# Moving the low parts of the first layer's inner values, group 0, from GpSimd to VectorE

## The chip, the cores and the metric

The kernel runs on one core of a Trainium2 chip. A core has five engines that work side by side, each through its own queue in order: TensorE (PE in the profile, with its weight loads as PEld), VectorE (DVE), ScalarE (ACT), GpSimd (POOL) and SyncE (SP), which here issues nearly all transfers. The metric is the device time of one execution in microseconds (us). Before the change it is 747.45 us, the median of three runs (747.26 to 748.68).

## The reference

Three stages follow each other on 1152 tokens of width 512:

```python
# attention: 2 batches, 8 heads, 576 positions, head width 64
scores = scale * q @ k.T
scores = where(scores >= max(scores) - tau, scores, -1e9)
x = softmax(scores) @ v                                   # laid out as 1152 x 512
# first layer: inner width 768
h = maximum(maximum(x @ w1, x @ w2), x @ w3)
x = h @ w_out
# experts: 4 of them, inner width 1024, weighted by normalised domain_probs
out = sum(p[:, e] * (maximum(x @ w1[e], 0) @ w2[e]) for e in range(4))
```

The change lies in the first layer: `h` is the "inner value" of its title.

## The kernel before

Every product is made from split operands. A 32-bit value `v` is cut into a high part `hi` (a copy in the type fp32r) and a low part `lo = v - hi`, and a product is the sum of three matrix products, `hi*lo`, `lo*hi` and `hi*hi` (`split_term`). So each weight block and each activation tile needs a copy (the high part, on ScalarE) and a subtraction (the low part).

The tokens are cut into two groups. Group 0 holds 512 tokens of batch 0, group 1 the other 640, worked in two halves of 320. The program runs attention on batch 0, then the layers of group 0 as one long stream of products (`Stream`), into which attention on batch 1 is woven towards the end of the first layer, then the layers of group 1.

In the first layer of group 0 the outer loop runs over six blocks `f` of 128 inner columns, and for each over the three weight matrices `i = 0, 1, 2`. One block of weights is 128x512 (four slices of 128x128) and takes 12 matrix products of 512 columns on TensorE; the first `f` is worked in two halves of 256 tokens. Then the output matrix follows, four output blocks `d` with two weight blocks of 128x384 each.

The weights come as 64-bit floats, and each block is turned into 32-bit by integer work in the same stretch (`block`): L648 loads the words; ScalarE scales the upper word (L656); GpSimd clamps it (L666, tile `b`); VectorE takes three bits of the lower word (L663), merges them with the clamped word (L669) and sets the sign (L674, tile `raw`). After that ScalarE copies the high part (L633, tile `a`), GpSimd makes the low part (L637, tile `a`), and SyncE keeps the 32-bit block in device memory for group 1 (L680). Four word tiles are in flight.

After each block of products, `after_max` takes the running maximum: for `i = 0` ScalarE copies the sums (L718), for `i = 1` and `2` VectorE takes the maximum of the new sums in PSUM and the old maximum in SBUF (L720, tile `hmax`). After `i = 2` two more steps follow: ScalarE copies the high part (L725, tile `hh`) and the low part is made from `hmax` and `hh` (L728, tile `hl`). Both `hmax` and `hh` lie in SBUF. The products with the output matrix read `hh` and `hl`.

What sets the order: weights' steps are planned at a lag, in columns of products, ahead of their use (`LAGS64`, `LAGS_FIRST`), and the steps after a block are put 1000 columns apart behind it (`AFTER`). In this stretch the engines' orders are those in which the stream calls the steps (`ordered`). When the last words have been used, their memory is given to attention on batch 1, whose first loads (`load_job`, L129 and L130) stand on SP's queue behind the last L680.

Of the kernel before, what the change touches and what calls it, by code (L numbers as in the profile page):

```python
# [14 lines left out]
ALU = mybir.AluOpType  # L15
# [6 lines left out]
def fused_kernel(ctx: ExitStack, tc: tile.TileContext, q, k, v, tau, w1, w2, w3, w_out, probs, m_w1, m_w2, out):  # L22
    nc = tc.nc
# [47 lines left out]
    def f32(ap):  # L71
        return ap.bitcast(F32)
# [365 lines left out]
    class Queue:  # L438
# [3 lines left out]
        def add(self, gen):  # L442
            self.q.append(gen)
# [164 lines left out]
    def htile(g, nm):  # L608
        return mo["h"].tile([P, GROUPS[g]["n"]], F32R, tag="h", name=nm, bufs=HB[g])

    def wtile(shape, dt, tag, bufs):
        return wp.tile(shape, dt, tag=tag, name=tag, bufs=bufs)
# [74 lines left out]
    def block64(w, cols):  # L687
        return w.bitcast(U32).rearrange("(k p) (f two) -> p k f two", p=P, two=2)[:, :, cols, :]

    def weights64(g, name, use, src, shape):  # L690
        kept["planned"] = kept.get("planned", 0) + 1
        return block(use, shape, "a", NA, None, (LAGS_FIRST if kept["planned"] <= EARLY else LAGS64, LAGS_KEPT)[g], name, g, src if g == 0 else None)
# [13 lines left out]
    def layer_max(g):  # L706

        G = GROUPS[g]
        hs = [None] * NF
        acc = {}  # L710

        def after_max(f, i, si, a, z):
            def first(ps):
                if hs[f] is None:
                    hs[f] = (htile(g, "hh"), htile(g, "hl"))
                new = wtile([P, z - a], F32, "hmax", 3)
                if i == 0:
                    nc.scalar.activation(out=new, in_=ps, func=AF.Copy)  # L718
                else:
                    nc.vector.tensor_tensor(out=new, in0=ps, in1=acc[si], op=ALU.max)  # L720
                acc[si] = new

            def hi(ps):
                acc["done", f, si] = acc[si]
                nc.scalar.activation(out=hs[f][0][:, a:z], in_=acc[si], func=AF.Copy)  # L725

            def lo(ps):
                nc.gpsimd.tensor_tensor(out=hs[f][1][:, a:z], in0=acc["done", f, si], in1=f32(hs[f][0][:, a:z]), op=ALU.subtract)  # L728

            return [first, hi, lo] if i == 2 else [first]  # L730

        for f in range(NF):

            halves = [(0, MAIN // 2), (MAIN // 2, MAIN)] if g == 0 and f == 0 else []
            bs = {}
            for i, (si, (a, z)) in [(i, s) for s in enumerate(halves) for i in range(3)] or [(i, s) for i in range(3) for s in enumerate(G["subs"])]:
                if i not in bs:
                    bs[i] = weights64(g, f"w{i}_{f}", plan.cols, block64((w1, w2, w3)[i], slice(f * P, (f + 1) * P)), [P, KC, P])
                add(z - a, KC, lambda j, b=bs[i], a=a, z=z: (
                    b["hi"][:, j, :], b["lo"][:, j, :], X[g][j][0][:, a:z], X[g][j][1][:, a:z]), after_max(f, i, si, a, z))  # L740
        K2 = NF // 2
        for d in range(KC):
            bs = []
            for i in range(2):
                src = block64(w_out[i * K2 * P:(i + 1) * K2 * P], slice(d * P, (d + 1) * P))
                bs.append(weights64(g, f"o{d}_{i}", plan.cols + i * 3 * K2 * G["subs"][0][1], src, [P, K2, P]))
            for a, z in G["subs"]:
                def hi(ps, d=d, a=a, z=z):
                    if Y[g][d] is None:
                        Y[g][d] = tuple((xp0, xp1)[g].tile([P, G["n"]], F32R, tag="xy", name=f"y{g}{part}{d}", bufs=2 * KC) for part in "hl")  # L750
                    nc.scalar.activation(out=Y[g][d][0][:, a:z], in_=ps, func=AF.Copy)

                def lo(ps, d=d, a=a, z=z):
                    nc.vector.tensor_tensor(out=Y[g][d][1][:, a:z], in0=ps, in1=f32(Y[g][d][0][:, a:z]), op=ALU.subtract)

                add(z - a, NF, lambda j, bs=bs, a=a, z=z: (
                    bs[j // K2]["hi"][:, j % K2, :], bs[j // K2]["lo"][:, j % K2, :], hs[j][0][:, a:z], hs[j][1][:, a:z]), [hi, lo])
# [224 lines left out]
```

## Time and profile before

| | before |
|---|---|
| time, median of three runs | 747.45 us (747.26 to 748.68) |
| the profiled execution's own time | 746.17 us |
| its span, first to last instruction | 744.3 us |
| TensorE busy | 712.6 us, 96% of the span |
| VectorE busy | 378.7 us, 51% |
| ScalarE busy | 338.5 us, 45% |
| GpSimd busy | 392.2 us, 53% |
| mean granted TensorE clock | 0.991 of full speed |

The stretch that the change touches is 117 to 172 us of the span. The shares above are means over all stages and do not tell which engine sets the pace there. In rows of the timeline the first number is the start in us from the span's start, the second the time taken, then engine, line, operation, tiles (out<-in) and shapes; a bracket tells how long the engine had been idle before and what ended that.

### The profile page before, as it was taken

The numbers are of one execution on the slowest core, as the hardware profiler recorded it, in microseconds if no ns is written. First come the engines' busy times: TensorE is split into PE (matmuls) and PEld (weight loads), VectorE is DVE, ScalarE is ACT, GpSimd is POOL, SyncE is SP. The second block draws the span as 40 slices with busy tenths as digits, with TensorE's granted clock in tenths as the row PEclk, the third lists the DMA queues.
The fourth block names the chain that finished last, engine by engine and source line by source line (L and its number), as shares of the span: only waits on it lengthen the run. The fifth ranks groups of instructions, "written<-read, shape, count | busy, mean of one in ns | idle before, by whom it ended". The sixth has DMA issues, their size and how long they took to land.

```text
span 744.3 us, 11711 instructions
## 1 busy us (share of the span) xinstructions
PE 712.6 (96%) x4103; PEld 634.5 (85%) x4103; DVE 378.7 (51%) x900; ACT 338.5 (45%) x716; POOL 392.2 (53%) x435
## 2 busy tenths in 40 slices
PE   3888999999899999999999999999999999999997
PEld 3777899777788888888888899999998998998996
DVE  5889998775376766776767321112222222222222
ACT  5689884554554555464554423333321321322320
POOL 4689885777664564574464534554522522522520
PEclk8799999999999999999999999999999999999999
DMA  6342006877723224222221322213412312412403
GB/s 182 106 146 49 1 1 190 271 217 207 203 89 103 72 66 111 72 73 57 72 71 57 89 96 85 78 55 97 129 42 84 104 44 80 111 45 72 114 1 71
DMA packets 89369, 71.01 MB, mean 95 GB/s; under 512 B 24158, under 2 KB 75358, under 8 KB 89310
## 3 DMA queue, kind: packets, MB, share of 16 engines
q1 hardware_dynamic: 88860, 69.96, 32.7%
q8 instruction: 33, 0.54, 0.3%
q10 hardware_dynamic: 418, 0.30, 0.2%
q14 instruction: 26, 0.21, 0.1%
q0 software_dynamic: 32, 0.00, 0.0%
HBM read 61.59 MB, written 8.65 MB: 94 GB/s over the span
## 4 chain that ended last, share of the span: by engine, by line
PE 80%; DVE 5%; POOL 5%; issue 3%; ACT 3%; DMA 2%; SPq 1%; POOLq 0%; DVEq 0%; ACTq 0%
PE ps L842 64%; PE s L302 5%; PE u L419 5%; PE t L343 3%; POOL a L637 2%; PE u L176 1%; DVE st_negm L313 1%; DMA krem<-in_k_dram 1%; PE u L166 1%; DVE raw L674 1%; POOL b L666 1%; SPq L129 1%; ACT a L633 1%; DVE K L172 1%; PE t L389 1%
## 5 line engine op out<-in xcount | busy, mean ns | idle before, releaser
L637 POOL TENSOR_TENSOR a<-raw,a 128x512 fp32r<-128x512 f32 (+1 forms) x116 | 145.0, 1256 | 163.6 <-ACT a L633 160.3
L842 PE MATMUL ps<-b,hh 128*128 128x512 f32 x576 | 184.3, 392 | 0.0
L842 PEld LDWEIGHTS ps<-b,hh 128*128 128x128 f32 x576 | 107.3, 188 | 20.5
L792 ACT ACTIVATE hh<-ps 128x320 fp32r<-128x320 f32 (+1 forms) x96 | 46.8, 488 | 150.2 <-PE ps L842 149.8
L842 PE MATMUL ps<-b,hl 128*128 128x512 f32 x288 | 113.1, 393 | 0.0
L842 PE MATMUL ps<-y1h,a 128*128 128x320 f32 x512 | 112.8, 309 | 0.0
L637 POOL TENSOR_TENSOR b<-raw,b 128x512 fp32r<-128x512 f32 x64 | 82.9, 1296 | 51.4 <-ACT b L633 51.4
L795 DVE SCALAR_TENSOR_TENSOR hl<-ps,hh 128x320 fp32r<-128x320 f32 (+1 forms) x96 | 53.4, 557 | 107.1 <-ACT hh L792 107.0
L633 ACT ACTIVATE a<-raw 128x512 fp32r<-128x512 f32 (+1 forms) x116 | 69.5, 612 | 58.8 <-PE ps L842 22.9
L811 DVE SCALAR_TENSOR_TENSOR acc<-ps,pr,acc 128x512 f32<-128x512 f32 x63 | 47.2, 749 | 80.4 <-PE ps L842 80.3
L320 ACT ACTIVATE em<-s,st_negm 128x576 f32<-128x576 f32 x72 | 53.4, 743 | 73.1 <-DVE st_negm L313 72.9
L842 PEld LDWEIGHTS ps<-y1h,a 128*128 128x128 f32 x512 | 85.4, 188 | 0.3
L842 PE MATMUL ps<-y0h,a 128*128 128x512 f32 x256 | 83.9, 398 | 0.8 <-POOL a L637 0.8
L333 POOL TENSOR_SCALAR em<-em,st_r,even 128x576 f32<-128x576 f32 x70 | 57.6, 824 | 43.9 <-DVE st_r L332 42.2
L842 PE MATMUL ps<-y1l,a 128*128 128x320 f32 x256 | 79.1, 309 | 0.0
L313 DVE TENSOR_REDUCE st_negm<-s 128x1 f32<-128x576 f32 x72 | 54.2, 752 | 48.6 <-PE s L302 48.2
L302 PE MATMUL s<-K,QS 128*128 128x288 f32 x320 | 59.4, 313 | 7.0 <-DVE st_thr L316 3.1
L842 PE MATMUL ps<-x1h,a 128*128 128x320 f32 x288 | 63.4, 309 | 0.0
L325 DVE SCALAR_TENSOR_TENSOR em<-s,st_thr,em 128x576 f32<-128x576 f32 x72 | 58.3, 812 | 8.7 <-ACT em L320 6.9
L842 PEld LDWEIGHTS ps<-b,hl 128*128 128x128 f32 x288 | 54.1, 188 | 9.9
L302 PEld LDWEIGHTS s<-K,QS 128*128 128x128 f32 x320 | 49.5, 196 | 11.9 <-issue 6.0
L842 PEld LDWEIGHTS ps<-y0h,a 128*128 128x128 f32 x256 | 47.0, 188 | 9.4 <-POOL a L637 1.2
(129 smaller groups left out, 1268.8 us busy)
## 6 DMA issues: line engine op xcount, KB each, us to landing
raw<-in_moe_w_dram SPq DMA_DIRECT2D x128, 256.0 KB
words<-in_moe_w_dram SPq DMA_DIRECT2D x18, 512.0 KB
kept_w<-raw SPq DMA_DIRECT2D x18, 256.0 KB
raw<-kept_w SPq DMA_DIRECT2D x18, 256.0 KB
kraw<-in_k_dram SPq DMA_DIRECT2D x30, 128.0 KB
words<-in_moe_w_out_dram SPq DMA_DIRECT2D x8, 384.0 KB
vraw<-in_v_dram SPq DMA_DIRECT2D x8, 256.0 KB
qraw<-in_q_dram SPq DMA_DIRECT2D x7, 256.0 KB
```

Of the source, the lines that this page charges most:

```text
L302: nc.tensor.matmul(st.s[:, kh, 0:HS], lhsT=l, rhs=r, start=i == 0, stop=i == len(terms) - 1)
L313: nc.vector.tensor_reduce(out=st.stat["negm"], in_=views(st)[0], op=ALU.max, axis=AX.XY, negate=True)
L320: return nc.scalar.activation(out=ev, in_=sv, func=AF.Exp, bias=st.stat["negm"])
L325: nc.vector.scalar_tensor_tensor(out=ev, in0=sv, scalar=st.stat["thr"], in1=ev, op0=ALU.is_ge, op1=ALU.mult, accum_out=st.stat["sum"])
L333: last = (nc.vector if swift else nc.gpsimd).tensor_scalar(out=em, in0=em, scalar1=re, scalar2=even, op0=ALU.mult, op1=ALU.add)
L419: at["valued"] = nc.tensor.matmul(pv, lhsT=l, rhs=r, start=i == 0, stop=i == len(terms) - 1)
L633: nc.scalar.activation(out=b["hi"], in_=b["raw"], func=AF.Copy)
L637: nc.gpsimd.tensor_tensor(out=b["lo"], in0=b["raw"], in1=f32(b["hi"]), op=ALU.subtract)
L792: nc.scalar.activation(out=hs[f][0][:, a:z], in_=ps, func=AF.Relu)
L795: nc.vector.scalar_tensor_tensor(out=hs[f][1][:, a:z], in0=ps, scalar=0.0, in1=f32(hs[f][0][:, a:z]), op0=ALU.max, op1=ALU.subtract)
L811: nc.vector.scalar_tensor_tensor(out=accs[t], in0=ps, scalar=pe, in1=accs[t], op0=ALU.mult, op1=ALU.add)
L842: nc.tensor.matmul(ps, lhsT=l, rhs=r, start=i == 0, stop=i == count - 1)
```

## The change

The subtraction on L728 is issued on VectorE for group 0 (`g` is 0) and stays on GpSimd for group 1.

```diff
             def lo(ps):
-                nc.gpsimd.tensor_tensor(out=hs[f][1][:, a:z], in0=acc["done", f, si], in1=f32(hs[f][0][:, a:z]), op=ALU.subtract)
+                (nc.gpsimd if g else nc.vector).tensor_tensor(out=hs[f][1][:, a:z], in0=acc["done", f, si], in1=f32(hs[f][0][:, a:z]), op=ALU.subtract)
```

Seven instructions move: two of 128x256 for the first `f` and five of 128x512. The orders of TensorE, ScalarE and SyncE stay as they are. Numbers behind a name tell the buffers apart: `words_1972` is the third weight block of `f = 2`, `raw_2099` its 32-bit form, `hmax_2096` the finished maximum of `f = 1`.

On VectorE, at the end of `f = 1`, this stands before the change:

```order
L669 SCALAR_TENSOR_TENSOR bits_2085<-b_2060,bits_2085 128x512
L720 TENSOR_TENSOR hmax_2096<-ps_2062,hmax_2065 128x512
L674 SCALAR_TENSOR_TENSOR raw_2099<-words_1972,bits_2085 128x512
L663 TENSOR_SCALAR bits_2118<-words_2013 128x512
L669 SCALAR_TENSOR_TENSOR bits_2118<-b_2091,bits_2118 128x512
L674 SCALAR_TENSOR_TENSOR raw_2134<-words_2013,bits_2118 128x512
L663 TENSOR_SCALAR bits_2151<-words_2047 128x512
L669 SCALAR_TENSOR_TENSOR bits_2151<-b_2124,bits_2151 128x512
L720 TENSOR_TENSOR hmax_2162<-ps_2126,hmax_2131 128x512
```

And this at the same place on VectorE after it:

```order
L669 SCALAR_TENSOR_TENSOR bits_2085<-b_2060,bits_2085 128x512
L720 TENSOR_TENSOR hmax_2096<-ps_2062,hmax_2065 128x512
L674 SCALAR_TENSOR_TENSOR raw_2099<-words_1972,bits_2085 128x512
L728 TENSOR_TENSOR hl_2033<-hmax_2096,hh_2032 128x512
L663 TENSOR_SCALAR bits_2118<-words_2013 128x512
L669 SCALAR_TENSOR_TENSOR bits_2118<-b_2091,bits_2118 128x512
L674 SCALAR_TENSOR_TENSOR raw_2134<-words_2013,bits_2118 128x512
L663 TENSOR_SCALAR bits_2151<-words_2047 128x512
L669 SCALAR_TENSOR_TENSOR bits_2151<-b_2124,bits_2151 128x512
L720 TENSOR_TENSOR hmax_2162<-ps_2126,hmax_2131 128x512
```

L728 now stands on VectorE's queue behind the L674 that closes a block and in front of the conversion of the next three blocks.

On GpSimd, around the same L728, this stands before the change:

```order
L637 TENSOR_TENSOR a_2081<-raw_2068,a_2073 128x512
L666 TENSOR_SCALAR b_2091<-b_2091 128x512
L728 TENSOR_TENSOR hl_2033<-hmax_2096,hh_2032 128x512
L637 TENSOR_TENSOR a_2114<-raw_2099,a_2104 128x512
L666 TENSOR_SCALAR b_2124<-b_2124 128x512
```

And this on GpSimd after it:

```order
L637 TENSOR_TENSOR a_2081<-raw_2068,a_2073 128x512
L666 TENSOR_SCALAR b_2091<-b_2091 128x512
L637 TENSOR_TENSOR a_2114<-raw_2099,a_2104 128x512
L666 TENSOR_SCALAR b_2124<-b_2124 128x512
L637 TENSOR_TENSOR a_2147<-raw_2134,a_2139 128x512
```

The low part of the weight block `raw_2099` and the clamp of `b_2124` no longer stand behind L728.

On ScalarE nothing moves: the copy `hh_2032`, which L728 reads, stands directly behind the copy `a_2104` of `raw_2099`, the tile that the L674 in the rows of VectorE makes.

## Rows read from the trace of the kernel before

**Rows 1.** Waits, 126 to 162 us: who waited for whom, us in total, times, longest

```profile
PEld ps L842 <- POOL a L637: 3.5, 4, 1.0
PE ps L842 <- POOL a L637: 1.9, 4, 0.5
```

**Rows 2.** Timeline of PE, 117 to 200 us

```profile
168.87 0.50 PE L842 MATMUL ps<-hl,a 128*128 128x512 f32 x1 [1.59 <-POOL hl L728]
...
189.31 0.51 PE L842 MATMUL ps<-y0l,a 128*128 128x512 f32 x1 [1.29 <-ACT a L633]
```

**Rows 3.** Timeline of ACT, DVE and POOL, 129 to 139 us

```profile
129.50 0.68 DVE L674 SCALAR_TENSOR_TENSOR raw<-words,bits 128x512 uint32<-128x512 uint32 x1
...
130.09 0.69 DVE L663 TENSOR_SCALAR bits<-words 128x512 uint32<-128x512 uint32 x1
...
130.29 0.63 ACT L633 ACTIVATE a<-raw 128x512 fp32r<-128x512 f32 x1 [1.41 <-POOL b L666]
...
130.83 0.62 ACT L725 ACTIVATE hh<-hmax 128x512 fp32r<-128x512 f32 x1
...
131.53 1.31 POOL L728 TENSOR_TENSOR hl<-hmax,hh 128x512 fp32r<-128x512 f32 x1 [1.24 <-ACT hh L725]
...
132.22 0.69 DVE L663 TENSOR_SCALAR bits<-words 128x512 uint32<-128x512 uint32 x1
...
132.78 1.29 POOL L637 TENSOR_TENSOR a<-raw,a 128x512 fp32r<-128x512 f32 x1
...
134.04 0.62 POOL L666 TENSOR_SCALAR b<-b 128x512 f32<-128x512 f32 x1
...
134.69 0.69 DVE L669 SCALAR_TENSOR_TENSOR bits<-b,bits 128x512 uint32<-128x512 uint32 x1 [1.79 <-POOL b L666]
...
138.49 0.68 DVE L674 SCALAR_TENSOR_TENSOR raw<-words,bits 128x512 uint32<-128x512 uint32 x1
```

**Rows 4.** Waits of DVE, 117 to 172 us

```profile
DVE bits L669 <- POOL b L666: 9.3, 7, 1.9
DVE hmax L720 <- ACT hmax L718: 0.7, 1, 0.7
DVE bits L669 <- DVE bits L663: 0.5, 1, 0.5
```

**Rows 5.** Instructions of L754: duration ns min/median/max, first and last start

```profile
L754 DVE TENSOR_TENSOR y0l<-ps,y0h x4: 691/692/693, 171.2 to 182.8; 128x512 fp32r<-128x512 f32 x4
```

**Rows 6.** Timeline of DVE and POOL, 104.9 to 108.2 us

```profile
105.00 0.57 DVE L333 TENSOR_SCALAR em<-em,st_r,even 128x576 f32<-128x576 f32 x1
105.15 0.90 POOL L393 TENSOR_SCALAR am<-tcopy 128x512 fp32r<-128x512 f32 x1
```

**Rows 7.** Instructions of L393: duration ns min/median/max, first and last start

```profile
L393 POOL TENSOR_SCALAR am<-tcopy x15: 614/621/895, 30.7 to 105.1; 128x512 fp32r<-128x512 f32 x15
```

**Rows 8.** Timeline around the two half-width L728 and the last one, 117 to 168 us

```profile
117.56 0.40 ACT L725 ACTIVATE hh<-hmax 128x256 fp32r<-128x256 f32 x1
117.56 0.69 DVE L674 SCALAR_TENSOR_TENSOR raw<-words,bits 128x512 uint32<-128x512 uint32 x1
117.74 1.29 POOL L637 TENSOR_TENSOR a<-raw,a 128x512 fp32r<-128x512 f32 x1 [6.57 <-ACT a L633]
...
121.88 0.69 DVE L663 TENSOR_SCALAR bits<-words 128x512 uint32<-128x512 uint32 x1
...
122.60 0.40 ACT L725 ACTIVATE hh<-hmax 128x256 fp32r<-128x256 f32 x1
...
166.83 0.63 ACT L725 ACTIVATE hh<-hmax 128x512 fp32r<-128x512 f32 x1 [0.69 <-DVE hmax L720]
167.18 0.55 DVE L663 TENSOR_SCALAR bits<-words 128x384 uint32<-128x384 uint32 x1
```

**Rows 9.** Timeline of ACT and DVE, 175 to 190 us

```profile
175.81 0.54 DVE L674 SCALAR_TENSOR_TENSOR raw<-words,bits 128x384 uint32<-128x384 uint32 x1
...
186.60 0.63 ACT L247 ACTIVATE V<-vraw 128x512 fp32r<-128x512 f32 x1 [3.13 <-DMA vraw<-in_v_dram]
```

## The prediction

> **What bounds the kernel now.** TensorE is the engine that sets the end, so I first read what it waits for in the stretch that the change touches. Between 126 and 162 us there are four stalls, one for each block `f` from 2 to 5, all ended by GpSimd's L637, 1.9 us on the matmul row and 3.5 us on the weight-load row [rows 1]. A fifth, 1.59 us, ends with L728 itself at 168.87, and a sixth, 1.29 us, comes at 189.31 when attention on batch 1 begins [rows 2].
>
> Next I read the timeline of one turn of the loop [rows 3]. The reader is to see three things. GpSimd's L728 starts at 131.53 and stands in front of the L637 at 132.78 for which TensorE waits. The clamp L666 follows at 134.04, and VectorE's L669 at 134.69 has waited 1.79 us for it. And VectorE's L674 starts at 129.50 and again at 138.49: a turn takes 8.99 us. So GpSimd's queue, held up by L728's wait for `hh`, makes VectorE late, and this is repeated each turn. Over 117 to 172 us VectorE waits 9.3 us for clamps in seven waits, 0.7 us for L718 and 0.5 us at one more L669 [rows 4].
>
> **What it removes.** L728 leaves GpSimd: 1.31 us per turn and the wait in front of it [rows 3]. L637 can then start when its copy L633 ends, at 130.29 + 0.63 = 130.92, with 0.08 us for the semaphore at 131.00 instead of 132.78. The clamp comes as much earlier, so VectorE's clamp waits should go. An unhindered L669 starts 0.10 us after the L663 that it depends on, so of nine waits of 9.3 + 0.7 + 0.5 = 10.5 us, 9 x 0.10 stay and 9.6 us are won on VectorE's queue [rows 4].
>
> **What it adds.** On VectorE a subtraction of 128x512 takes 0.69 us [rows 5] and the next instruction can start 0.60 us after its start, as from 129.50 to 130.09 [rows 3]. But L728 needs `hh`, and VectorE's queue has nothing to do in between. `hh` stands on ScalarE behind the L633 that copies the block that VectorE's own L674 has just made: L674 129.50 to 130.18, L633 from 130.29 (the trace names GpSimd there, but it is the end of L674 that this copy needs), L725 130.83 to 131.45 [rows 3]. L728 can start at 131.48, and the L663 behind it at 132.08 instead of 130.09: 1.99 us later. Queued behind it are the conversions of the next three weight blocks, for which ScalarE, GpSimd and then TensorE wait, and the maxima L720.
>
> At the three other full-width places inside the loop the same offsets repeat, so four times 1.99 = 7.96 us. At the first half-width place `hh` ends at 117.56 + 0.40 = 117.96 and the L674 behind L728 starts at 117.99 + 0.34 = 118.33 instead of 117.56, 0.77 us; at the second `hh` ends at 123.00 and L663 starts at 123.37 instead of 121.88, 1.49 us; at the last `hh` ends at 167.46 and L663 starts at 168.09 instead of 167.18, 0.91 us [rows 8]. The sum is 11.13 us. Against 9.6 us won, VectorE ends this stretch 1.5 us later than before: the wait for GpSimd is replaced by a wait for ScalarE that is a little longer.
>
> **A price that the trace shows only for a neighbour.** At 131.48, when L728 would start on VectorE, GpSimd's L637 is running from 131.00 to 132.29. VectorE's other instructions of this stretch have an operand in PSUM and keep their length beside GpSimd; L728 has both inputs and its output in SBUF. The nearest rows are of an instruction with all data in SBUF: VectorE's L333 at 105.00, 0.57 us, and beside it GpSimd's L393 took 0.90 us [rows 6]. Of 15 such L393 the median is 0.62 us and this one, 0.895, is the longest [rows 7]. So the two shut each other out for about 0.27 us there. It is a one-input instruction; one with two inputs in SBUF beside GpSimd is not in the trace. The bounds are therefore zero (both run on) and the full rest of GpSimd's instruction. I take the full rest, because the row nearest in kind shows exclusion.
>
> The Trainium skill, page "SBUF — State Buffer", section "SBUF: two separate sides", states a port pair shared by VectorE and GpSimd, an exclusive lock held for the whole instruction, which a VectorE instruction with two SBUF inputs also needs against a GpSimd instruction that reads SBUF. By it L728 waits until L637 has ended; the trace agrees for the one-input kind with the 0.895 against 0.62 us above, and no run shows the other kind yet.
>
> With exclusion L728 gets through at 132.29, and I let the next instruction start 0.52 us later (0.60 less 0.08 us of start-up spent while it waited): 132.81 instead of 132.08, 0.73 us more, four times 2.92 us. At the first half-width place L637 runs to 119.03 [rows 8], so L674 starts at 119.03 + 0.26 = 119.29, 0.96 us more. At the second the L633 in front of `hh` ends 0.09 us after `hh` starts, as in the loop, so L637 runs from 122.77 to 124.06 and L663 starts at 124.32, 0.95 us more. At the last place no L637 is running: the one before it has long ended, the next comes after. Together 4.83 us, and VectorE is 1.5 + 4.8 = 6.3 us later at the end of the stretch. A turn would take 8.99 - 1.69 + 1.99 + 0.73 = 10.0 us. The clamps that are held up by up to 0.6 us stay hidden, since VectorE reaches their L669 more than 3 us after L728.
>
> **What sets the end.** VectorE's last L674 of the stretch, at 175.81, releases the last L680 and, behind it on SP's queue, the loads of attention on batch 1. Their values arrive at 186.60 on ScalarE, and behind that copy stands the L633 that ends TensorE's stall at 189.31 [rows 2, 9]. So a delay of VectorE's last conversion arrives there nearly whole, and the gains on TensorE before it (no more waits for L637 behind L728, 0.6 us at 168.87) only lengthen that stall. From there on TensorE is busy with few gaps, so the delay reaches the end: span 744.30 + 6.3 = 750.6 us, with the 1.87 us that lie outside the span (746.17 - 744.30) 752.5 us for the profiled execution. The median of the runs is 1.28 us above it: **753.8 us**.
>
> **Rivals.** Without exclusion the sum is 1.5 us: 749.0 us, with 0.6 us either way for the offsets that I repeated from one turn. For it speaks that the only rows of exclusion are of another kind of instruction; against it, that L728's operands are all in SBUF. It decides if L728 ends about 0.7 us after `hh`.
>
> Faster: L728's wait is hidden, because `hh` comes within the 0.6 us that L674 takes. Then the five stalls of [rows 1] and [rows 2] go, 3.5 + 1.6 = 5.1 us by the weight-load row, and with VectorE 9.6 us ahead the loads for batch 1 come earlier too: 742.3 us. It is GpSimd's 1.31 against VectorE's 0.69 us that speaks for it; against it speaks ScalarE's order, where `hh` stands behind a copy that itself needs that L674. The Trainium skill, page "GPSIMD Engine Reference", section "Performance versus the Vector engine", advises VectorE for elementwise work as about twice as fast; on the bare durations the trace agrees (1.31 against 0.69 us).
>
> No change: the loads of batch 1 are not tied to the last L674 but to other transfers, so that only TensorE's own delay is left: without exclusion at most the 1.5 us less the 0.62 us by which L728 is shorter on VectorE (1.31 - 0.69), 0.9 us or 748.3 us. Against it, the last L680 stands directly in front of those loads on SP's queue. The change does happen: the order shows L728 on the other queue.
>
> **How the numbers follow.** Forecast with exclusion 0.58, its own range 752 to 755.3; without exclusion 0.28; no change 0.08; faster 0.06. A difference of 0.2%, 1.5 us, is about what a measurement can tell from none. Without exclusion the sum lies on that border, so half of it is slower and half the same: slower 0.58 + 0.15 = 0.73, same 0.13 + 0.08 = 0.21, faster 0.06. The range reaches from 748.2, below the case without exclusion, to 755.3 us, 1.5 us above the forecast, for clamps that are held up and would not be hidden after all.
>
> **What would show it.** In the changed profile L728 on VectorE takes, or waits, until L637 ends on GpSimd: recorded at about 1.3 us with exclusion, 0.69 us without. The step from L674 to L674 is 10.0 us (9.3 without exclusion, under 8.5 in the faster case). VectorE's waits for L666 are gone and a wait for L725 stands in their place. TensorE's waits for L637 in the loop grow, and the stall at 189.31 comes about 6 us later. Wrong would be a step below 8.99 us, or a last L674 that is late while attention on batch 1 is not.

## The result, and the profile after

The changed kernel is slower. Its median is 755.76 us (754.92 to 756.65, 4 runs) against 747.79 us of the kernel before in the same comparison (747.26 to 748.68): ratio 1.0113, 95% interval 1.0091 to 1.0134. The forecast of 753.8 us had the sign and, as far as VectorE's last conversion, the mechanism; the measured median lies 0.46 us above the top of its range. The profiled execution took 756.65 us with a span of 754.7 us, 10.4 us more than the span before; the median moved by 8.0 us. So this one execution lies 0.9 us above its own median, and the two figures are kept apart below.

One turn of the loop on ScalarE, VectorE and GpSimd in the changed kernel (start, duration, engine, line, tiles, and in brackets the idle time before the instruction and what ended it):

```profile
132.10 0.68 DVE L674 SCALAR_TENSOR_TENSOR raw<-words,bits 128x512 uint32<-128x512 uint32 x1
...
132.89 0.64 ACT L633 ACTIVATE a<-raw 128x512 fp32r<-128x512 f32 x1 [1.40 <-POOL b L666]
...
133.43 0.62 ACT L725 ACTIVATE hh<-hmax 128x512 fp32r<-128x512 f32 x1
133.61 1.30 POOL L637 TENSOR_TENSOR a<-raw,a 128x512 fp32r<-128x512 f32 x1 [0.72 <-ACT a L633]
...
134.08 1.37 DVE L728 TENSOR_TENSOR hl<-hmax,hh 128x512 fp32r<-128x512 f32 x1 [1.30 <-ACT hh L725]
...
134.87 1.06 POOL L666 TENSOR_SCALAR b<-b 128x512 f32<-128x512 f32 x1
135.37 0.68 DVE L663 TENSOR_SCALAR bits<-words 128x512 uint32<-128x512 uint32 x1
```

Set it beside [rows 3]. L637 no longer stands behind L728: it starts 0.08 us after the end of its L633, as foretold. VectorE now sits idle 1.30 us until `hh` is there, then needs 1.37 us for a subtraction that takes 0.69 us elsewhere, and its next L663 starts 135.37 - 132.10 = 3.27 us after the L674, not 0.59 us as before. L637 ends at 134.91, L728 0.54 us later, at 135.45. GpSimd's L666, which starts beside L728 at 134.87, takes 1.06 us instead of the 0.62 us of [rows 3]: each of the two engines holds the other up.

VectorE's waits from 117 to 180 us (who waited for whom, us in total, times, longest), the answer to [rows 4]:

```profile
DVE hl L728 <- ACT hh L725: 7.0, 7, 1.3
DVE y0l L754 <- ACT y0h L751: 0.7, 1, 0.7
```

The 9.3 us for clamps are gone and 7.0 us for `hh` stand in their place. TensorE's waits for L637 have become longer, since the weights come later. From 117 to 180 us there are five where [rows 1] counts four, the fifth behind the loop (before the change the same 63 us hold no others than those four):

```profile
PE ps L842 <- POOL a L637: 4.0, 5, 0.9
PEld ps L842 <- POOL a L637: 5.6, 5, 1.2
```

Behind the loop, the answer to [rows 9] and [rows 2]: VectorE's last L674, the values of batch 1 on ScalarE, and TensorE's stalls.

```profile
174.35 0.50 PE L842 MATMUL ps<-hl,a 128*128 128x512 f32 x1 [1.99 <-DVE hl L728]
...
182.54 0.55 DVE L674 SCALAR_TENSOR_TENSOR raw<-words,bits 128x384 uint32<-128x384 uint32 x1
...
192.08 0.63 PE L166 MATMUL u<-ident,kraw 128*128 128x128 f32 x4 [1.10 <-DMA kraw<-in_k_dram]
...
194.32 0.63 ACT L247 ACTIVATE V<-vraw 128x512 fp32r<-128x512 f32 x1 [4.70 <-DMA vraw<-in_v_dram]
...
197.08 0.80 PE L842 MATMUL ps<-y0l,a 128*128 128x512 f32 x1 [2.26 <-ACT a L633]
198.42 0.80 PE L842 MATMUL ps<-y0h,a 128*128 128x512 f32 x1 [0.55 <-POOL a L637]
```

The last L674 is 6.73 us later than in [rows 9], the values 7.72 us. The stall for L728 in front of the output matrix has grown from 1.59 us [rows 2] to 1.99 us. The stall before the third product of the experts has grown from 1.29 to 2.26 us, and the first matmul behind it takes 0.80 us instead of 0.51 us. Why that matmul is longer is seen in the granted clock, the eighth column from the left of the busy times by stretch (stretch, its length, busy time of PE, PEld, DVE, ACT and POOL with counts, granted TensorE clock as a share of 2.4 GHz, DMA share, GB/s). The changed kernel:

```profile
185.00:190.00 5.00, 5.00 (x24) 4.14 (x23) 0.69 (x1) 2.74 (x6) 4.67 (x5) 1.00 0.66 188
190.00:195.00 5.00, 3.71 (x18) 2.48 (x16) 0.00 (x0) 0.63 (x1) 1.19 (x4) 1.00 0.77 202
...
197.00:200.00 3.00, 2.37 (x5) 1.47 (x6) 1.29 (x2) 2.95 (x8) 2.74 (x4) 0.50 0.83 233
200.00:205.00 5.00, 5.00 (x19) 4.09 (x18) 0.87 (x2) 2.02 (x7) 2.92 (x3) 0.62 0.52 161
```

The kernel before, in the same 5 us:

```profile
200.00:205.00 5.00, 5.00 (x27) 4.21 (x26) 1.97 (x3) 1.12 (x2) 1.60 (x2) 1.00 0.64 145
```

After a stretch with TensorE's stalls the granted clock stands at 1.2 GHz from 197 to about 204 us: TensorE is busy all the time from 200 to 205 us and does 19 instructions where it did 27. TensorE is 7.8 us later than before when the clock falls, 10.2 us when it is back at 2.4 GHz, and stays at 10.2 to 10.4 us to the last instruction.

### The profile page after: what moved, and what is told of

The parts are those of the page before. It is cut to its first block, busy times and chain, and to the rows that moved or that the text cites. A ratio compares the mean times of both kernels' runs of the same rounds, so it can differ in the third digit from the quotient of the medians.

```text
span 754.7 us, 11711 instructions
## 1 busy us (share of the span) xinstructions
PE 717.0 (95%) x4103; PEld 635.9 (84%) x4103; DVE 387.0 (51%) x907; ACT 340.0 (45%) x716; POOL 386.8 (51%) x428
## 4 chain that ended last, share of the span: by engine, by line
PE 77%; DVE 8%; ACT 5%; issue 3%; DMA 3%; POOL 2%; SPq 2%; DVEq 0%; ACTq 0%; POOLq 0%
PE ps L842 62%; PE u L419 5%; PE s L302 4%; PE t L343 3%; DVE raw L674 1%; DVE st_negm L313 1%; DVE hl L728 1%; DVE bits L663 1%; DVE bits L669 1%; SPq L129 1%; PE u L176 1%; ACT a L633 1%; DVE hmax L720 1%; DMA words<-in_moe_w_dram 1%; ACT em L320 1%
## 5 line engine op out<-in xcount | busy, mean ns | idle before, releaser
L637 POOL TENSOR_TENSOR a<-raw,a 128x512 fp32r<-128x512 f32 (+1 forms) x116 | 145.0, 1255 | 180.1 <-ACT a L633 176.7
L637 POOL TENSOR_TENSOR b<-raw,b 128x512 fp32r<-128x512 f32 x64 | 82.8, 1294 | 54.6 <-ACT b L633 54.3
L633 ACT ACTIVATE a<-raw 128x512 fp32r<-128x512 f32 (+1 forms) x116 | 69.7, 614 | 63.9 <-DVE raw L674 21.2
L842 PE MATMUL ps<-y0h,a 128*128 128x512 f32 x256 | 85.7, 406 | 0.6 <-POOL a L637 0.6
```

What stands on the lines that cost most here:

```text
L633: nc.scalar.activation(out=b["hi"], in_=b["raw"], func=AF.Copy)
L637: nc.gpsimd.tensor_tensor(out=b["lo"], in0=b["raw"], in1=f32(b["hi"]), op=ALU.subtract)
L842: nc.tensor.matmul(ps, lhsT=l, rhs=r, start=i == 0, stop=i == count - 1)
```

## Experiments

My theory: VectorE's queue waits for `hh` (2.0 us a turn), then for GpSimd's L637 (0.7 us a turn), and its lateness goes to the end. Rivals: no exclusion; VectorE has no room for the seven subtractions at all; the end is set by something else. VectorE's lateness is measured in each trace as the time from the start of the first L720 to the start of the last L674, called the stretch below, so that noise from the attention stage in front of it drops out. The first L720 before the change and after it:

```profile
114.27 0.42 DVE L720 TENSOR_TENSOR hmax<-ps,hmax 128x256 f32<-128x256 f32 x1 [0.36 <-PE ps L842]
...
114.77 0.43 DVE L720 TENSOR_TENSOR hmax<-ps,hmax 128x256 f32<-128x256 f32 x1 [0.37 <-PE ps L842]
```

The stretch is 61.54 us in the kernel before (114.27 to 175.81) and 67.77 us in the changed one (114.77 to 182.54): 6.23 us more. "Step" is the time of one turn, from the L674 that closes a block `f` to the next such L674. All ratios are to the kernel before on the same chip.

### One part at a time: exclusion, the wait, the place

e1, the third maximum goes to PSUM, so that L728 reads one input there:

```
-                new = wtile([P, z - a], F32, "hmax", 3)
+                new = ps if i == 2 and g == 0 else wtile([P, z - a], F32, "hmax", 3)
```

> Edit against the changed kernel: in the first group the third maximum (L720) is written over the matmul's own tile in PSUM instead of into an SBUF tile, so L725 and L728 read it from PSUM. L728 stays on VectorE, every engine keeps its order, and L728 still waits for hh. Theory (exclusion between L728 and GpSimd's L637 costs 0.73 us a turn and 4.8 us in all): L728 128x512 takes about 0.7 us instead of 1.37, the step from L674 to L674 falls from 9.98 to 9.3 us, VectorE's last L674 comes 4.8 us earlier (177.7 instead of 182.5 us), and the time falls from 755.8 by 4.8 to about 751 us, by up to 2.4 us more (748.6) if the stretch at 1.2 GHz behind TensorE's long stall goes with it. Rival (no exclusion; an instruction with two SBUF inputs waits or is long for another reason, or the wait for hh is all that matters): step stays 9.9 to 10.0 us and time 755 to 756 us. Second rival: the PSUM tile is held until L728 has read it, 2 us longer, and TensorE waits for a tile: then new PE waits released by L728 stand in front of the first matmul of a product, and the time stays above 753 us.

Measured: 750.24 us (7 runs), ratio 1.0041 (1.0026 to 1.0057). L728 runs beside L637 and keeps its length:

```profile
130.96 1.30 POOL L637 TENSOR_TENSOR a<-raw,a 128x512 fp32r<-128x512 f32 x1 [0.72 <-ACT a L633]
...
131.40 0.69 DVE L728 TENSOR_TENSOR hl<-ps,hh 128x512 fp32r<-128x512 f32 x1 [1.26 <-ACT hh L725]
```

The step is 9.26 us and the stretch 62.85 us, 1.31 us more than before (the prediction's sum without exclusion was 1.5). Exclusion thus costs 6.23 - 1.31 = 4.92 us, foretold 4.83. A small part of it may belong to the copy L725, which now reads PSUM too and is 0.04 us shorter in a turn (0.58 us). This agrees with the rule of the Trainium skill, "SBUF — State Buffer", section "SBUF: two separate sides", cited in the prediction: the rule names two inputs in SBUF, and with one of them in PSUM L728 kept its 0.69 us beside L637. The second rival, a TensorE that waits for the longer held PSUM tile, is not seen: the time is under 753 us, and the only stall of TensorE's matmuls for L728 is the one in front of the output matrix (1.96 us), which the changed kernel has as well. The time, however, is 2.9 us above the kernel before, not 1.3.

e2, `hh` in front of the L633 on ScalarE; L728 on VectorE:

```
+            def both(ps):
+                first(ps)
+                hi(ps)
...
-            return [first, hi, lo] if i == 2 else [first]
+            if i < 2:
+                return [first]
+            return [first, hi, lo] if g else [both, lambda ps: None, lo]
```

> Edit against the changed kernel: in the first group L725 (hh) is issued on ScalarE directly behind the third maximum, in front of the L633 that needs VectorE's L674; L728 stays on VectorE at the same place. Theory (the loss comes from where hh stands on ScalarE: VectorE's queue waits 1.3 us a turn for it and then meets GpSimd's L637): L728 starts within 0.15 us of the end of the L674 before it, ends before L637 starts, takes 0.69 us, and the turn is set by TensorE (8.2 to 8.6 us). VectorE's last L674 comes 6 to 9 us earlier than in the changed kernel and the time is 742 to 746 us, faster than the kernel before (747.8). Rival (VectorE has no room for the seven subtractions themselves, wait or not): step 9.3 us or more and time 752 us or more.

Measured: 745.14 us (12 runs), ratio 0.9972 (0.9959 to 0.9985). In the loop L728 follows its L674 without a wait and is through before L637 starts:

```profile
129.36 0.68 DVE L674 SCALAR_TENSOR_TENSOR raw<-words,bits 128x512 uint32<-128x512 uint32 x1
129.48 0.64 ACT L725 ACTIVATE hh<-hmax 128x512 fp32r<-128x512 f32 x1 [0.73 <-DVE hmax L720]
...
130.15 0.69 DVE L728 TENSOR_TENSOR hl<-hmax,hh 128x512 fp32r<-128x512 f32 x1
...
130.87 1.29 POOL L637 TENSOR_TENSOR a<-raw,a 128x512 fp32r<-128x512 f32 x1 [0.71 <-ACT a L633]
```

The step is 8.1 us, the stretch 58.22 us, 9.55 us less than in the changed kernel, where 6 to 9 were foretold. VectorE has room for the seven subtractions; what it lacked was `hh`.

e3, L728 on VectorE behind the next block's L669 (three empty steps in front of `lo`), and e4, L728 on GpSimd behind L637 (one empty step, the kernel before otherwise):

```
+            late = [lambda ps: None] * 3 if g == 0 else []
-            return [first, hi, lo] if i == 2 else [first]
+            return [first, hi] + late + [lo] if i == 2 else [first]
```

> Edit against the changed kernel: L728 stays on VectorE and is issued three steps later, behind the next block's L663 and L669 instead of in front of them. Theory (wait for hh and meeting L637 are the loss, not the 0.69 us): hh has been ready for about 1 us when L728's turn comes, no wait for L725 stands on VectorE, the step is 8.3 to 8.8 us, and the time is 742 to 747 us; the last hl comes later than before (the stall of TensorE in front of the second layer, 1.99 us in the changed kernel, may grow to 3 us). If L728 meets the L666 on GpSimd instead, that L666 or L728 takes up to 0.6 us more. Rival (VectorE's own time is the loss): 9.3 us or more a turn and 752 us or more.

> Edit against the kernel before: L728 stays on GpSimd and is issued one step later, behind the L637 for which TensorE waits instead of in front of it. Theory (what bounds the kernel before is L637 standing behind L728's wait for hh): L637 starts at once when L633 ends, 1.8 us earlier in a turn; TensorE's four stalls for L637 between 126 and 162 us (3.5 us) go; the clamp L666 comes 0.4 us earlier; step 8.4 to 8.7 us; time 743 to 746 us against 747.8. Rival (the end is set by VectorE's conversions alone and these by the clamp, which hardly moves): step 8.9 us or more, time within 1.5 us of the kernel before.

Measured: e3 746.57 us (12 runs), ratio 0.9997 (0.9987 to 1.0007); e4 746.16 us (12 runs), 0.9991 (0.9979 to 1.0002). Both steps are as foretold (8.46 and 8.47 us). The times gain less: e3's is at the slow end of its range, e4's is 0.2 us above its range and within the 1.5 us of the kernel before that its rival gave, and both intervals include no change at all. VectorE's stretch is only 0.40 us shorter than before in e3, where L728 met GpSimd in every turn (1.36 to 1.37 us again), and 2.33 us in e4, where the median fell by 1.2 us.

e8, `hh` first as in e2, but L728 on GpSimd (`nc.gpsimd` in `lo`):

> Edit against the kernel before: L728 stays on GpSimd; only hh (L725) is issued on ScalarE directly behind the third maximum, in front of the L633. It tells what of the gain of hh first (745.1 us with L728 on VectorE) is owed to the order on ScalarE alone. L728 can start at about 130.4 in the turn from 129.5 instead of 131.5 and ends at 131.7, so L637 starts 1.1 us earlier (131.7 instead of 132.8) and the clamp as well. Theory (order is what counts): step from 8.99 to 8.2 to 8.5 us, time 744.5 to 746.5 us, within 1.5 us of the kernel with L728 on VectorE. Rival (the engine counts: 0.69 us on VectorE against 1.31 us on GpSimd in front of L637): step 8.7 us or more, 746.5 us or more.

Measured: 742.09 us (6 runs), ratio 0.9938 (0.9924 to 0.9952), the fastest of all, and 2.4 us faster than foretold at least: both theories had given GpSimd too little. On the same chip e7, which is e2 with nine products more on TensorE (below), took 743.45 us, 1.4 us longer; e2 itself was compared on another chip. GpSimd does L728 and L637 back to back:

```profile
128.66 0.63 ACT L725 ACTIVATE hh<-hmax 128x512 fp32r<-128x512 f32 x1
...
129.39 1.31 POOL L728 TENSOR_TENSOR hl<-hmax,hh 128x512 fp32r<-128x512 f32 x1
...
130.64 1.31 POOL L637 TENSOR_TENSOR a<-raw,a 128x512 fp32r<-128x512 f32 x1
```

The stretch is 57.23 us. So with `hh` first the move to VectorE costs 1 us of the stretch again. The Trainium skill, "GPSIMD Engine Reference", section "Performance versus the Vector engine", holds for the duration (0.69 against 1.31 us), not for the place: here the slower engine had the free time.

e9 looks for that microsecond: e2 with the two half-width L728 of f = 0 back on GpSimd (`nc.gpsimd if g or f == 0 else nc.vector`):

> Edit against the kernel with hh first and L728 on VectorE (2.2 us faster than the kernel before): the two half-width L728 of the first block (f = 0) go back to GpSimd, the five others stay on VectorE. In that kernel's trace the first of the two takes 1.33 us on VectorE instead of 0.42, because L637 is running, and the L674 behind it starts at 119.06 us instead of 117.29 in the kernel with hh first and L728 on GpSimd; the five others take 0.69 us and meet no L637. Theory (what is left of the change once hh comes first is this one meeting, and the clock behind a longer stall): VectorE's last L674 comes 0.7 to 1.2 us earlier (171.1 to 171.6 us), and the time is 3.5 to 5 us below the kernel before, as with L728 on GpSimd (4.6 below). Rival (the subtractions on VectorE cost something at the other places too): last L674 within 0.3 us of 172.3, time 2 to 3 us below the kernel before.

Measured: 744.44 us (9 runs), ratio 0.9965 (0.9951 to 0.9980). The stretch is 57.45 us, 0.77 us less than in e2 and 0.22 us more than in e8: on VectorE's queue the one meeting with L637 was most of the cost. The two signs that I had set, however, came out as the rival said. The last L674 stands at 172.46 us; that is because this execution came to its first L720 at 115.01 us instead of 114.08. The time is 2.6 us below the kernel before, not 3.5 to 5, which is hardly more than e2's 2.2. So the 0.77 us are shown on VectorE's queue and not in the time, and why e8 is faster than both is not shown.

### Behind the stretch: lateness alone, and the clock

e5, the kernel before with VectorE held up by work done again:

```
+                    for _ in range(10 if (g, f, i) == (0, NF - 1, 1) else 1):
                         nc.vector.tensor_tensor(out=new, in0=ps, in1=acc[si], op=ALU.max)
...
+            for _ in range(4 if kept["signs"] == 26 else 1):
...
```

> Edit against the kernel before: L728 stays on GpSimd; VectorE is made late by repeating work that it does anyway, with the same result: the second maximum of the last block is issued ten times (9 x 0.60 = 5.4 us) and the last L674 four times (3 x 0.47 = 1.4 us); 1.1 us of it goes into waits that VectorE has there. Theory (the whole loss of the changed kernel is VectorE's lateness, and behind it the loads of batch 1 and the clock): the last L674 ends about 5.7 to 6.5 us later than in the kernel before, the values of batch 1 reach ScalarE 6 to 7.5 us later, the granted clock falls to 1.2 GHz behind TensorE's stall, and the time is 753.5 to 756.5 us, as in the changed kernel (755.8). Rival (a part of that loss comes from L728's move itself: shorter GpSimd work, other meeting of transfers, a busier port): 751 us or less although the last L674 is as late.

Measured: 756.10 us (4 runs), ratio 1.0129 (1.0112 to 1.0145). The time was met, but by a delay that I had sized wrongly: the repeats of the maximum came 0.72 us apart and those of the L674 0.59, so the stretch grew by 10.4 us, not 6. It shows that lateness of VectorE reaches the end without L728's move (9.4 us more for 10.4), and it took from the theory the 8.0 us: at this rate 6.23 us of lateness are worth an estimated 5.6. It is no copy of the changed kernel otherwise: TensorE's stall for L728 is 8.13 us there, not 1.99.

e6 and e7, nine products in TensorE's stall, in the changed kernel and in e2:

```
+                    for _ in range(9 if x == 27 and i == 0 else 0):
+                        nc.tensor.matmul(ps, lhsT=Y[0][0][0][:, 0:P], rhs=Y[0][0][0][:, 0:n], start=True, stop=True)
```

> Edit against the changed kernel: nine products of 128x512, whose result is written over, are put on TensorE where it stands idle for 2.26 us before 197.08 us; they need 9 x 0.226 = 2.0 us of the 2.26. Theory (about 2.4 us of the loss in the profiled run is the stretch at 1.2 GHz that follows this stall): the granted clock stays at 2.4 GHz behind it, and the time falls from 755.8 to 753 to 754.3 us. Rival (the clock falls for another reason, or what it costs is given back in later waits): the stretch at 1.2 GHz stays, or it goes and the time stays within 0.7 us of 755.8. Second rival: the nine products delay the real ones, and the time grows by up to 2 us.

> Edit against the kernel with hh first and L728 on VectorE (745.1 us): the same nine products in the same stall, which there is 2.31 us long before 186.50 us. Theory (clock): TensorE's start in front of attention on batch 1, 3.85 us earlier than in the kernel before, shrinks to 1.2 us at the end only because of the stretch at 1.2 GHz; with it gone the time is 742.5 to 744 us, faster than all kernels so far. Rival: later waits take the gain back, 745 us.

Measured: e6 752.91 us (5 runs), ratio 1.0080 (1.0064 to 1.0096); e7 743.45 us (6 runs), 0.9958 (0.9941 to 0.9974). In neither trace does the clock fall behind the filled stall. e7 is within its range, but its 1.1 us against e2 lie between two comparisons whose intervals overlap. e10 puts five products into the kernel before, and e11 and e12 run the changed kernel and e6 side by side:

> Edit against the kernel before: five products of 128x512 (5 x 0.226 = 1.1 us), whose result is written over, in the stall of 1.29 us before 189.31 us; L728 on GpSimd. It asks if the kernel before loses time to the clock behind that stall as well. Theory (it does so in few of its runs, since its stall is short; its profiled run shows none): time within 0.7 us of the kernel before, so that the 1.8 us which nine products won in the changed kernel belong to the change. Rival (the same 1.8 us are won here): then the clock is no part of the difference, and 1.8 us of the loss are unexplained.

> The changed kernel itself, as the measure for the next run on the same chip: so far it and the kernel with nine products in the stall were compared only through the kernel before on two chips, with intervals that touch (1.0091 to 1.0134 and 1.0064 to 1.0096). Expected: 7 to 8.5 us above the kernel before; the stretch on VectorE from the first L720 to the last L674 is 67.8 us again; a stretch at 1.2 GHz behind the stall before the third product of the experts.

> The changed kernel with nine products of 128x512 in TensorE's stall, on the same chip as the changed kernel itself. Theory (the clock behind that stall is a term of its own): 1.0 to 2.4 us faster than the changed kernel in the same call, no stretch at 1.2 GHz behind the stall, and what is left against the kernel before is VectorE's 6.2 us. Rival (the difference seen before was one between chips): within 0.7 us of the changed kernel.

Measured: e10 746.28 us (12 runs), ratio 0.9994 (0.9983 to 1.0006); e11 752.61 us (6 runs), 1.0075 (1.0059 to 1.0091); e12 752.56 us (6 runs), 1.0075 (1.0061 to 1.0089). e10 is 0.8 us below the kernel before, where 0.7 was the bound, and its interval includes no change. e11 missed two of its three expectations: the changed kernel itself loses only 5.4 us here, and its trace shows no stretch at 1.2 GHz behind that stall. The nine products bring nothing in the median, so the gain that I gave to e6 was a difference between comparisons, and the rival of e12 held. In what two executions of the same program differ is seen in the timeline of its second trace:

```profile
172.79 0.50 PE L842 MATMUL ps<-hl,a 128*128 128x512 f32 x1 [1.99 <-DVE hl L728]
...
180.99 0.55 DVE L674 SCALAR_TENSOR_TENSOR raw<-words,bits 128x384 uint32<-128x384 uint32 x1
...
191.34 0.63 ACT L247 ACTIVATE V<-vraw 128x512 fp32r<-128x512 f32 x1 [2.31 <-DMA vraw<-in_v_dram]
...
194.05 0.51 PE L842 MATMUL ps<-y0l,a 128*128 128x512 f32 x1 [0.48 <-ACT a L633]
```

and in its busy times by stretch:

```profile
172.00:180.00 8.00, 7.21 (x25) 5.75 (x25) 6.74 (x13) 3.97 (x10) 4.59 (x7) 0.79 0.58 195
...
197.00:200.00 3.00, 3.00 (x16) 2.43 (x15) 1.38 (x3) 2.38 (x7) 2.89 (x3) 1.00 0.56 174
```

The stretch is 67.77 us again, to the hundredth. But its first L720 came at 113.22 us (114.77 in the first trace), the values follow the last L674 after 10.35 us (11.78), and the clock fell behind the earlier stall, at 174 us (0.79 in that row), where TensorE's later start only shortened the next stall to 0.48 us. It stayed at 2.4 GHz behind that one.

Where the time between the last L674 and the values goes is seen on SyncE, which issues a batch's loads one after the other behind the last L680. One pair of `kraw` loads and the load of the values before the change (first two rows) and after it:

```profile
178.03 1.37 SPq L129 DMA_DIRECT2D kraw<-in_k_dram  x2
...
182.62 0.75 SPq L129 DMA_DIRECT2D vraw<-in_v_dram  x1
...
184.75 2.26 SPq L129 DMA_DIRECT2D kraw<-in_k_dram  x2
...
190.32 0.75 SPq L129 DMA_DIRECT2D vraw<-in_v_dram  x1
```

The load of the values is issued 6.13 us after the last L680 before the change (176.49), 7.10 us after it in the changed kernel (183.22) and 5.89 us after it in e11; from this issue to the copy on ScalarE it is 3.98, 4.00 and 3.79 us. So the longer time lies in the issues, most of it in this pair. In the other eleven traces the values follow the last L674 after 10.0 to 11.5 us (11.14 in e10, 11.46 in e2), so these 10.35 to 11.78 us are not shown to be an effect of the change.

The profiled executions together. Columns: stretch on VectorE; start of the values' copy against the 186.60 us of the kernel before; span against its 744.3 us; the difference of these two; time at 1.2 GHz behind the stall before the third product.

| kernel | stretch | values | span | span less values | at 1.2 GHz |
|---|---|---|---|---|---|
| changed | 67.77 | +7.7 | +10.4 | 2.7 | 6.8 |
| e11 changed, again | 67.77 | +4.7 | +4.9 | 0.2 | none |
| e12 changed, filled | 67.78 | +6.1 | +6.2 | 0.1 | none |
| e6 changed, filled | 67.80 | +5.4 | +5.7 | 0.3 | none |
| e1 max in PSUM | 62.85 | +1.6 | +4.4 | 2.8 | 6.8 |
| e10 before, filled | 61.57 | +0.2 | +0.4 | 0.2 | none |
| e3 VectorE, later | 61.14 | -1.4 | -1.4 | 0.0 | none |
| e4 GpSimd, later | 59.21 | -1.9 | 0.0 | 1.9 | 3.4 |
| e7 hh first, filled | 58.25 | -3.3 | -3.2 | 0.1 | none |
| e2 hh first | 58.22 | -2.8 | -1.2 | 1.6 | 3.4 |
| e9 hh first, f = 0 GpSimd | 57.45 | -3.3 | -0.3 | 3.0 | 6.8 |
| e8 hh first, GpSimd | 57.23 | -4.9 | -4.3 | 0.6 | none |
| e5 delay alone | 71.96 | +9.9 | +11.4 | 1.5 | 3.4 |

With no stretch at 1.2 GHz there, the span moves as the values do, within 0.6 us; with one the end comes a further 1.5 to 3.0 us later. So in these 14 executions what is added between the values and the end goes with the clock behind this stall. That is a match over traces and not a test: in the one pair that was run side by side for it, e11 and e12, the clock stayed up without the nine products too.

## Why the prediction was wrong, point by point

**What held.** L728's wait for `hh` behind L633; the clamp waits that go (9.6 us) against it (11.13 us), 1.5 us foretold and 1.31 measured in e1; exclusion, 4.83 foretold and 4.92 measured; together 6.3 against 6.23 us, the same in four traces. The step is 9.98 us (132.10 to 142.08), foretold 10.0. L728 beside L637 is recorded at 1.37 us, and the last one, which meets none, at 0.69. So "the full rest of GpSimd's instruction" was the right end of the bounds, and e1 refutes the rival without exclusion.

**The step that failed** is the last: "So a delay of VectorE's last conversion arrives there nearly whole" and "From there on TensorE is busy with few gaps, so the delay reaches the end". Two terms are missing in it. The loads between the last L674 and the values took 10.79 us in the kernel before and 10.35 and 11.78 us in two executions of the changed kernel; I took them as fixed. And the stall that I foretold to lengthen was costed at its own length, without the clock behind it: where it fell there, 1.5 to 3.0 us were added (2.7 in the profiled execution), although TensorE was busy. The profiled execution: 0.5 (earlier stage) + 6.23 + 0.99 (11.78 - 10.79) + 2.7 = 10.4 us. In the second one, e11, the same terms are -1.05 + 6.23 - 0.44 + 0.2 = 4.9 us: the first and the third can have either sign. The 0.6 us that I had TensorE gain at 168.87 did not come either, since that stall grew by 0.4 us; it is no part of the sum.

**Luck in the size of the miss.** The working ends at 752.5 us for a profiled execution, and the profiled execution took 756.65 us, 4.1 us more. The median misses by only 2.0 us because of the 1.28 us that I added for the way from the profiled execution to the median: it holds for the kernel before, while the changed kernel's profiled execution lies 0.9 us above its median.

**The range** was too short above for the same reason. Its 1.5 us stood for clamps held up on GpSimd; these were held up (1.06 us) and VectorE waited for none. They should have stood for the loads and the clock, some 1 us either way and up to 3 us. The second comparison (752.61 us, +5.4) lies in the range, the first (+8.0) outside.

**What stays open.** How often the clock falls behind this stall in runs without a profile: their mean clock (0.987 to 0.991) doesn't tell where. So the 2.6 us between the two comparisons of the same program are explained for the two profiled executions only; the two intervals touch (1.0091), and whether the chip has a part in it isn't shown. Why SyncE's issues take longer one time than the next wasn't tried.

**The rival "faster"** named the right lever: with `hh` in time the waits of [rows 1] and the wait for L728 of [rows 2] go, as e2 shows (none of TensorE's matmuls waits for L728 there). The other stall of [rows 2] does not: it is 2.31 us in e2. It took a swap on ScalarE, and GpSimd was then the better engine (e8 against e7).

## What to carry to other kernels

Before work is moved to a faster engine, look at where its input is made: an instruction that must wait holds up the whole queue behind it, and swapping the producer with its neighbour (e8, 0.9938) was worth more than the faster engine. A VectorE subtraction with both inputs in SBUF should not be timed to meet a GpSimd subtraction (1.37 us instead of 0.69 here); one input in PSUM avoided it in e1. A stall of TensorE that a change lengthens is to be priced with the granted clock behind it, as a range (0 to 3 us here).

## What the runs showed that I had not expected

- L728 ends 0.54 us after L637 at 128x512 (135.45 and 134.91 us) and 0.28 us after it at 128x256 in e2 (119.14 and 118.86 us), against 0.69 and 0.42 us alone: from these times most of its work is done once GpSimd's instruction has ended, so its recorded length (1.37 and 1.33 us) tells when the two met rather than its width.
- Repeating an instruction with the same inputs and the same output costs more than its place in a mixed queue: in e5 the L720 come 0.72 us apart, while in the loop the next instruction starts 0.60 us after an L720. Why wasn't tried.
- Two executions of one program reached the first L720 1.55 us apart (113.22 and 114.77 us), before the change can act.
